# State-space scan and gated feed-forward: where chunks 2 to 5 apply their masked products, and who rearranges C

## The chip, the cores and the metric

The kernel runs on one core of a Trainium2 chip. The metric is the device time of one execution, in microseconds; the time before is the median of three runs. Engines are named as in the profile: PE (TensorE; PEld are its weight loads), DVE (VectorE), ACT (ScalarE), POOL (GpSimd), SP (the engine that issues most DMAs).

## The reference, cut to what matters

Inputs: x (4 batches, 8 heads, 768 positions, 32 wide), a decay a for each batch, head and position, B and C (16 states for each position), and two weight matrices of the feed-forward part (256 x 2048 and 2048 x 256). Everything is float32.

```python
for c in range(nc):                       # chunks along the sequence
    cum = np.cumsum(la, axis=-1)          # la = log(clip(a))
    L = np.exp(cum[:, :, :, None] - cum[:, :, None, :]) * causal
    M = np.einsum('bhin,bhjn->bhij', Cc, Bc) * L
    y_intra = np.einsum('bhij,bhjd->bhid', M, xc)
    y_inter = np.einsum('bhin,bhnd->bhid', Cc, state) * np.exp(cum)[:, :, :, None]
    y[:, :, sl] = y_intra + y_inter
    state = decay_full * state + np.sum(Bx, axis=2)
...
h = x @ w_in          # x: y with its heads side by side, 3072 x 256
g = h * np.cos(h)
out = g @ w_out
```

y of a position is the sum of two parts: what comes from earlier positions of its own chunk, through the causal matrix M, and what comes from the state at the chunk's start.

## The kernel before, in words

**Tiling.** The sequence is cut into six chunks of 128 positions (NC = 6, P = 128), for all four batches at once. Chunks 0 and 1 are done as four units of 64 positions by other functions (`finish0`, `inner`, `weights`); chunks 2 to 5 are done by `turn2`, `intra2`, `masked`, `open2` and `finish2`. The feed-forward part takes each chunk in 16 steps (NF = 16); step n belongs to chunk n // 16.

**A step.** The main loop runs over n. `first(n)` (L725) multiplies 128 features by y into PSUM as hp; `wind` and `gate` (L732, L738, L747) make the cosine on ACT and DVE; `gated` (L752) multiplies it with hp on DVE into gT, and `differ` (L777, L779, L780) forms three differences of gT on POOL. `second(n - 2)`, which is `seven` (L834) from chunk 1 on, multiplies the gT and the differences of two steps before by w_out in seven matmuls. So PE alternates the first of step n with the second of step n - 2. Each engine works through its instructions in the order in which the loop writes them, and semaphores join the engines where a tile is written by one and used by another.

**The scan within the steps.** While the feed-forward part of chunk c - 1 runs, the scan of chunk c is worked in at fixed steps of it (`plan`). Counted from the first step of chunk c - 1: at steps 7 and 11, `turn2` prepares B and C for the two pairs of batches; a step later `intra2` (L621) makes C times B on PE; `masked` (L640) multiplies it on DVE with the decays and writes the masked matrix m, one tile for each batch (`m_at`). m of a batch is 128 rows j (the position that gives) by 8 heads by 128 columns i (the position that receives). The quarter in which j lies in the later half and i in the earlier is never written: it would be zero. The halves of j are laid out so that for the second batch of a pair (s = 1) they change places. The last masked product is written in step 13.

At the end of step 14 `open2` (L651, L659) lays down in the two y tiles the state times C, and in y[0] also the sums from which the next state comes. In step 15, behind the first of that step, `finish2` (L675) adds m times x in two passes: the late columns i over all 128 rows, then the early columns over the 64 rows that count. Then ACT copies y to yT (L682), which the first of step 16 reads, and `carry` (L697 on DVE, L701 on POOL) makes the next state.

**PSUM.** y, g (the result of `intra2`) and a few others share two pairs of banks (tag "scan"). `open2` takes the banks that g held, so it waits for `masked` to have read them.

**Shared tiles.** The tiles `ms` hold other things before chunk 2: parts of them are `lead`, `along1`, `reach1`, `own` and the weights m of the units of chunks 0 and 1.

**The head.** At the start, C of chunk 0 is loaded by four DMAs of the ACT queue as c4. POOL copies it to c0 with its dimensions in another order (L365), PE transposes c0 in four blocks (L417), ACT evicts them (L421) and takes B's transposes behind (L432), and PE makes the first products from them (L478), which DVE multiplies by the decays (L487).

Of the kernel before, what the change touches and what calls it, by code (L numbers as in the profile page):

```python
# [25 lines left out]
def kernel(  # L26
# [13 lines left out]
    V, ACT, G, PE = nc.vector, nc.scalar, nc.gpsimd, nc.tensor  # L40

    NB, H, S, D = x.shape
    N = B.shape[-1]
    P = 128
# [9 lines left out]
    W = P // 2  # L54
# [22 lines left out]
    raw, arow, along, blocks = {}, {}, {}, {}  # L77
# [41 lines left out]
    c4 = both[0][:, 1].rearrange("p (h r) n -> p h r n", h=H)  # L119
# [77 lines left out]
    def load_along(c, seqs=range(NB)):  # L197
# [5 lines left out]
        for b in seqs:  # L203
            for q in range(4 if b % 2 else 1):
# [9 lines left out]
                      in_=a[:, :, 0:P].rearrange("b h (k i) -> (b h) k i", k=2))  # L214
# [85 lines left out]
    for s in range(2):  # L300
# [3 lines left out]
        out=a_in, in_=a.rearrange("(u b) h (c p) -> (b h c) u p", u=NU, p=P))  # L304
# [52 lines left out]
    for p in range(2):  # L357
# [4 lines left out]
                  in_=mine.unsqueeze(2).to_broadcast([P, H, N]))  # L362
    c0 = loads.tile([P, 2, 2, 4, 2, N], FP32, tag="blocks", name="c0").rearrange(
        "p a b c d n -> p (a b c d n)").rearrange("p (r h n) -> p r h n", r=4, h=H)
    G.tensor_copy(out=c0.rearrange("p r h n -> p h r n"), in_=c4)  # L365
    G.memset(lead, 0.0)
    G.memset(lead[:, :, 0:1], 1.0)
    slot = const.tile([P, 2], FP32, name="slot")
# [5 lines left out]
    scaled, lam, reach, state, part, yT = {}, {}, {}, {}, {}, {}  # L374
# [252 lines left out]
    def masked(c, b):  # L627

        u, s = divmod(b, 2)
        g, ms = part[c, u][0:2]  # L630
        l = lam.pop((c, b))
        m = m_at[b]
        first = slice(s * W, s * W + W)
        for q in range(2):
            g_ = g[q][:, ::(-1 if s else 1), s * 2 * P:(s + 1) * 2 * P].rearrange(
                "p k (t i) -> p k t i", t=2)
            m_, l_ = (t[:, q * HH:(q + 1) * HH].rearrange("p (k t) i -> p k t i", k=2)
                      for t in (m, l))
            for js, is_ in ((slice(0, P), slice(W, P)), (first, slice(0, W))):
                V.tensor_tensor(out=m_[js, :, :, is_], in0=g_[js, :, :, is_],  # L640
                                in1=l_[js, :, :, is_], op=ALU.mult)
        ms.append(m)

    def open2(c):

        ys[c] = y = [pair("y") for _ in range(2)]
        for u in range(2):
            for s in range(2):
                for q in range(4):
                    r, p = group(q, s), 64 * (q % 2)  # L650
                    PE.matmul(y[s][p:p + 64, q // 2, u * P:(u + 1) * P],  # L651
                              lhsT=state[c - 1, u][r, s].rearrange("p t d -> p (t d)"),
                              rhs=part[c, u][2][r, s], start=(u == 0), stop=False,
                              tile_position=(r.start, p), skip_group_check=True)
        for b in range(NB if c < NC - 1 else 0):
            x_, sc = raw[c][1], scaled.pop((c, b))
            for q in range(4):
                two_, r = slice(2 * q, 2 * q + 2), group(q, b)
                PE.matmul(y[0][r, 0, (4 + b) * W:(5 + b) * W],  # L659
                          lhsT=sc[:, two_].rearrange("p h n -> p (h n)"),  # L660
                          rhs=x_[:, b, two_].rearrange("p h d -> p (h d)"), start=False, stop=True,
                          tile_position=(0, r.start), skip_group_check=True)

    def finish2(c):

        xr, y = raw[c][1], ys.pop(c)
        for late in (1, 0):
            i = slice(W, P) if late else slice(0, W)
            for u in range(2):
                for t in range(2):  # L670
                    for s in range(2):
                        b, m = 2 * u + s, part[c, u][1][s]
                        js = slice(0, P) if late else slice(s * W, s * W + W)
                        for q in range(4):
                            PE.matmul(y[s][32 * q:32 * q + 32, t, u * P + i.start:u * P + i.stop],  # L675
                                      lhsT=xr[js, b, 4 * t + q], rhs=m[js, 4 * t + q, i],
                                      start=False, stop=True, tile_position=(js.start, 32 * q),
                                      skip_group_check=True)
        yT[c] = two.tile([P, 2, TB], FP32, tag="yT", name="yT")
        to_ = yT[c].rearrange("p t (u s i) -> p t s u i", u=2, s=2)  # L680
        for s in range(2):
            ACT.copy(out=to_[:, :, s],  # L682
                     in_=y[s][:, :, 0:2 * P].rearrange("p t (u i) -> p t u i", u=2))
        for u in range(2):
            del part[c, u]
            if c < NC - 1:
                carry(c, u, y[0][:, 0, 4 * W:].rearrange("p (u s d) -> p u s d", u=2, s=2)[:, u])
# [228 lines left out]
    take_s0, _ = finish0(0)  # L916
# [74 lines left out]
    def pairs(n):  # L991

        return [(c, u) for c, at, _, turn_at, _, _ in plan for u in turn_at
                if at + turn_at[u] == n]
# [9 lines left out]
    def ends(n):  # L1004
        return [(c, us) for c, at, us, _, _, end in plan if at + end == n]
# [61 lines left out]
    for n in range(AHEAD, NC * NF + LAG):  # L1067
        c, f = divmod(n, NF)
        if n < NC * NF:

            if c > 0 and f == (NJ if c == 1 else 0):
                if c == 1:
                    load(2, only=(x,))
                load(c + 2)
            if n in (NF - 4, NF + 1):
                for b in range(2):
                    load_a(2, (2 * (n > NF) + b,))
                    load_along(2, (2 * (n > NF) + b,))
            first(n)
            wind(n)  # L1080
            for at in pairs(n):
                turn2(*at)
            for k in units_at(n, 2):
                turn_unit(k)
            if n + 1 in piece:
                rests_of.append(grade(*piece[n + 1], later=True))
            gate(n)
            while len(rests_of) > (n == AHEAD):
                rest = rests_of.pop(0)
                if rest:  # L1090
                    rest()
            joins = n in piece and piece[n] in held
            if joins:
                join(*piece[n])

            behind = [lambda at=at: halved(*at) for at in halves_at(n)]
            behind += [lambda k=k, p=p: decays0(k, p) for k, at in unit_at.items()
                       for p in range(2) if at[0][p] == n]
            behind = [lambda at=(c, 2 * u + 1): masked(*at) for c, u in pairs(n - 2)] + behind
            behind = [lambda k=k: weights(k, 1) for k in units_at(n - 1, 3)] + behind  # L1100
            if not joins and behind:
                behind.pop(0)()
            gated(n)
            if add_s and (n == NF - 5 or units_at(n - 1, 4)):
                add_s()
                add_s = None
            for do in behind:
                do()
            if f not in (10, 11):
                for do in unsummed:  # L1110
                    do()
                unsummed.clear()
            for k, ((_, last_), *_) in unit_at.items():
                if last_ == n:
                    weigh0(k)
                    if k == 3:
                        units_of_decay()
        for i, js in differ_at.get(n, ()):
            differ_w(i, js)
        for c, _ in ends(n - 1):  # L1120
            finish2(c)
            raw.pop(c)
        if n == AHEAD + 1:
            second(AHEAD - LAG)
        if n >= LAG and n != AHEAD:
            second(n - LAG)
        for c, u in pairs(n - 1):
            intra2(c, u)
            masked(c, 2 * u)
        for k in units_at(n, 3):  # L1130
            for t in range(2):
                inner(k, t)
            weights(k, 0)
        for k in units_at(n, 4):
            take_s, add_s = finish0(k)
            take_s()
        for k in units_at(n, 1):
            reach_unit(k)
        for c, _ in ends(n):
            open2(c)  # L1140
        for c, u in pairs(n + 1):
            for b in (2 * u, 2 * u + 1):
                reaches(c, b)
                load_along(c + 1, (b,))
            turn_blocks(c, u)
        for at, (c, u) in block_loads.items():
            if at == n:
                loading = load_blocks(c, u)
            if at <= n < at + 6:
                next(loading)  # L1150
# [30 lines left out]
```

## Time and profile before

| what | us |
|---|---|
| median of 3 runs (370.49 to 370.82) | 370.5 |
| profiled execution, device time | 371.16 |
| profiled execution, span | 369.4 |
| PE busy | 362.5 |
| DVE busy | 276.9 |
| POOL busy | 213.4 |
| ACT busy | 172.2 |
| L675 PE, four chunks, by the chain | 4 x 1.82 |
| L365 POOL, the copy of C | 0.613 |

The granted clock of PE was 1.0 in the whole profiled execution. Busy times overlap: an engine's busy time says how much it had to do, and only the chain of work that ended last says which of it set the end. Matmul records overlap too, as PE works on several at once, so the time that a group takes is read from the start of its first record to the start of what follows. A float32 matmul leaves two records.

### The profile page before, as it was taken

How to read it: one execution, taken by the hardware profiler on the slowest of the kernel's cores; microseconds unless marked ns; L12 is line 12 of the kernel's file. 1: busy time of each engine (PE TensorE's matmuls, PEld its weight loads, DVE VectorE, ACT ScalarE, POOL GpSimd, SP SyncE). 2: the span in 40 equal slices, each digit the busy share in tenths (PEclk: the TensorE clock that was granted, in tenths of full speed). 3: DMA queues.
4: the chain of work that ended last, by engine and by line, in shares of the span. 5: the costliest groups of instructions: out<-in, count | busy, mean ns of one | idle time of the engine just before them, and what ended most of it. 6: DMA issues, size and time to landing. Idle time of an engine off the chain costs nothing.

```text
span 369.4 us, 9265 instructions
## 1 busy us (share of the span) xinstructions
PE 362.5 (98%) x3646; PEld 325.0 (88%) x3646; DVE 276.9 (75%) x451; ACT 172.2 (47%) x299; POOL 213.4 (58%) x336
## 2 busy tenths in 40 slices
PE   7999999999999999999999999999999999999995
PEld 5688888888999889899989999889999988999995
DVE  7789998578699857978876987776887783543463
ACT  2697766453445244354344344434434534444442
POOL 6567757579784456665446674544675344554451
PEclk9999999999999999999999999999999999999999
DMA  9996957257226736631055341020010010010011
GB/s 135 244 381 134 224 114 100 44 147 185 72 78 90 139 106 91 196 107 34 6 80 113 92 129 44 1 52 5 18 23 0 2 30 2 2 29 2 0 30 30
DMA packets 97708, 30.60 MB, mean 83 GB/s; under 512 B 71456, under 2 KB 93568, under 8 KB 97664
## 3 DMA queue, kind: packets, MB, share of 16 engines
q1 hardware_dynamic: 95376, 29.55, 35.0%
q10 hardware_dynamic: 2288, 0.46, 0.8%
q8 instruction: 29, 0.48, 0.5%
q14 instruction: 15, 0.12, 0.1%
HBM read 26.58 MB, written 3.34 MB: 81 GB/s over the span
## 4 chain that ended last, share of the span: by engine, by line
PE 92%; DVE 3%; ACT 2%; issue 1%; ACTq 0%; DVEq 0%
PE hp L725 43%; PE o L834 34%; PE o L796 6%; PE y L675 2%; PE g L621 2%; DVE mag L279 1%; PE g L478 1%; DVE lam L397 1%; PE warm L84 1%; PE y L651 1%; PE y L520 1%; DVE mag L281 1%; PE y L503 1%; DVE w L738 1%; PE a_ps L386 1%
## 5 line engine op out<-in xcount | busy, mean ns | idle before, releaser
L725 PE MATMUL hp<-yT,w_in 128*128 128x256 f32 x768 | 183.2, 382 | 0.4 <-DVE gT L752 0.3
L725 PEld LDWEIGHTS hp<-yT,w_in 128*128 128x128 f32 x768 | 139.4, 190 | 19.5 <-issue 2.3
L777 POOL TENSOR_TENSOR gd<-gT 128x256 f32<-128x256 f32 x79 | 59.9, 758 | 99.9 <-DVE gT L752 86.8
L747 ACT ACTIVATE w<-w,quarter 128x512 f32<-128x512 f32 x96 | 69.2, 721 | 84.4 <-DVE w L738 84.3
L738 DVE SCALAR_TENSOR_TENSOR w<-hp,k 128x512 f32<-128x512 f32 x96 | 65.8, 685 | 44.3 <-ACT k L732 43.9
L732 ACT ACTIVATE k<-hp 128x512 int32<-128x512 f32 x96 | 57.0, 594 | 83.2 <-PE hp L725 82.9
L752 DVE TENSOR_TENSOR gT<-hp,w 128x512 f32<-128x512 f32 x96 | 65.3, 680 | 33.2 <-ACT w L747 21.7
L834 PE MATMUL o<-words,gd 128*128 128x128 f32 x474 | 66.0, 275 | 0.0
L834 PEld LDWEIGHTS o<-words,gd 128*128 128x128 f32 x474 | 59.3, 192 | 0.3 <-POOL gd L779 0.2
L834 PEld LDWEIGHTS o<-w_out,gT 128*128 128x128 f32 x316 | 47.2, 191 | 4.2
L834 PE MATMUL o<-w_out,gT 128*128 128x128 f32 x316 | 48.4, 276 | 0.0
L779 POOL TENSOR_TENSOR gd<-gT,gd 128x128 f32<-128x128 f32 x79 | 44.0, 556 | 6.2
L780 POOL TENSOR_TENSOR gd<-gT,gd 128x128 f32<-128x128 f32 x79 | 43.3, 548 | 6.2
L580 DVE TENSOR_TENSOR_SCAN lam<-arow,unit 128x512 f32<-128x512 f32 x32 | 42.7, 1333 | 0.0
L834 PE MATMUL o<-words,gT 128*128 128x128 f32 x158 | 30.6, 275 | 0.0
L834 PE MATMUL o<-w_out,gd 128*128 128x128 f32 x158 | 30.5, 275 | 0.0
L796 PE MATMUL o<-w_out,gT 128*128 128x256 f32 x128 | 29.9, 379 | 0.0
L796 PEld LDWEIGHTS o<-w_out,gT 128*128 128x128 f32 x128 | 24.2, 190 | 3.3
L640 DVE TENSOR_TENSOR m<-g,lam 128x256 f32<-128x256 f32 x64 | 24.7, 414 | 0.4
L834 PEld LDWEIGHTS o<-words,gT 128*128 128x128 f32 x158 | 24.0, 192 | 0.0
L834 PEld LDWEIGHTS o<-w_out,gd 128*128 128x128 f32 x158 | 24.0, 192 | 0.0
L851 DVE TENSOR_TENSOR sum<-ps,sum 128x256 f32<-128x256 f32 (+1 forms) x27 | 16.7, 645 | 0.6
(111 smaller groups left out, 279.2 us busy)
## 6 DMA issues: line engine op xcount, KB each, us to landing
arow<-a_cut SPq DMA_DIRECT2D x16, 512.0 KB
words<-in_moe_w_in_dram SPq DMA_DIRECT2D x8, 512.0 KB
words<-in_moe_w_out_dram SPq DMA_DIRECT2D x8, 512.0 KB
out_dram<-sum SPq DMA_DIRECT2D x18, 128.0 KB
xr<-in_x_dram SPq DMA_DIRECT2D x16, 128.0 KB
xr<-in_x_dram SPq DMA_DIRECT2D x16, 64.0 KB
bc<-in_B_dram SPq DMA_DIRECT2D x15, 64.0 KB
arow<-a_cut SPq DMA_DIRECT2D x2, 256.0 KB
```

Of the source, the lines that this page charges most:

```text
L580: V.tensor_tensor_scan(out=lam[c, b][:, hs].rearrange("p h i -> p (h i)"), data0=rows_.rearrange("p h i -> p (h i)"), data1=unit[:, b % 2 ...
L640: V.tensor_tensor(out=m_[js, :, :, is_], in0=g_[js, :, :, is_], in1=l_[js, :, :, is_], op=ALU.mult)
L725: PE.matmul(to_[:, e], lhsT=w_in[:, k, fs], rhs=y[:, k], start=(k == 0), stop=(k == KT - 1), skip_group_check=True)
L732: ACT.activation(k, hp[n], AF.Copy, bias=0.25, scale=INV_2PI)
L738: V.scalar_tensor_tensor(out=w, in0=hp[n], scalar=INV_2PI, in1=k, op0=ALU.mult, op1=ALU.subtract)
L747: ACT.activation(cos, cos, AF.Sin, bias=quarter, scale=TWO_PI)
L752: V.tensor_tensor(out=gT[n], in0=hp.pop(n), in1=cos, op=ALU.mult)
L777: G.tensor_tensor(out=d[:, 0:2], in0=g[:, 1:2].to_broadcast([P, 2, P]), in1=g[:, 3::-3], op=ALU.subtract)
L779: G.tensor_tensor(out=d[:, 2], in0=g[:, 0], in1=d[:, 0], op=ALU.subtract)
L780: G.tensor_tensor(out=d[:, 3], in0=g[:, 2], in1=d[:, 2], op=ALU.subtract)
L796: PE.matmul(o[c, u][:, t], lhsT=g[:, 2 * e + t], rhs=w_out[:, 2 * j + e], start=(j == e == t == 0), stop=(j == NJ - 1 and e == 1), skip_gr ...
L834: PE.matmul(at[q], lhsT=a_[q], rhs=w[q], start=(j == 0 and q in starts), stop=(j == NJ - 1), skip_group_check=True)
```

## The change

The scan and the head are edited. In `finish2` the two passes of 64 matmuls of 64 columns become one pass of 32 matmuls of 128 columns over all 128 rows, zeros included; so that the unwritten quarter of m holds zeros, `masked` sets it to zero once, in chunk 2, by a POOL memset for each batch (the quarter is not written again by any later chunk). And `finish2` is called directly behind `open2`, at the end of step 14, in place of step 15. In the head, the copy from c4 to c0 is cut in two: POOL copies the first two of four blocks, ACT the other two.

```diff
-    G.tensor_copy(out=c0.rearrange("p r h n -> p h r n"), in_=c4)
+    G.tensor_copy(out=c0[:, 0:2].rearrange("p r h n -> p h r n"), in_=c4[:, :, 0:2])
+    ACT.copy(out=c0[:, 2:4].rearrange("p r h n -> p h r n"), in_=c4[:, :, 2:4])
...
         m = m_at[b]
+        if c == 2:
+            G.memset(m[W - s * W:P - s * W, :, 0:W], 0.0)
...
-        for late in (1, 0):
-            i = slice(W, P) if late else slice(0, W)
-            for u in range(2):
-                for t in range(2):
-                    for s in range(2):
-                        b, m = 2 * u + s, part[c, u][1][s]
-                        js = slice(0, P) if late else slice(s * W, s * W + W)
-                        for q in range(4):
-                            PE.matmul(y[s][32 * q:32 * q + 32, t, u * P + i.start:u * P + i.stop],
-                                      lhsT=xr[js, b, 4 * t + q], rhs=m[js, 4 * t + q, i],
-                                      start=False, stop=True, tile_position=(js.start, 32 * q),
-                                      skip_group_check=True)
+        for u in range(2):
+            for s in range(2):
+                for h in range(H):
+                    q, t = h % 4, h // 4
+                    PE.matmul(y[s][32 * q:32 * q + 32, t, u * P:(u + 1) * P],
+                              lhsT=xr[:, 2 * u + s, h], rhs=part[c, u][1][s][:, h],
+                              start=False, stop=True, tile_position=(0, 32 * q),
+                              skip_group_check=True)
...
-        for c, _ in ends(n - 1):
-            finish2(c)
-            raw.pop(c)
         if n == AHEAD + 1:
...
         for c, _ in ends(n):
             open2(c)
+            finish2(c)
+            raw.pop(c)
```

## The prediction

> **What bounds the kernel now.** I read the engines' rows of the page first, then the chain of work that ended last, then the timeline at one of the four places that are edited, then the head of the kernel.
>
> ```profile
> PE 362.5 (98%) x3646; PEld 325.0 (88%) x3646; DVE 276.9 (75%) x451; ACT 172.2 (47%) x299; POOL 213.4 (58%) x336
> PE 92%; DVE 3%; ACT 2%; issue 1%; ACTq 0%; DVEq 0%
> L675 PE MATMUL y<-m,xr x512: 212/219/243, 131.5 to 307.5; 128*32 128x64 f32 x86, 64*32 64x64 f32 x85
> ```
>
> TensorE is busy for 98% of the span and is 92% of the chain, so a change counts by what it does to the order and the seams of TensorE's work; other engines count only if TensorE comes to wait for them. The third line is the edited code: 512 records, 128 in each of chunks 2 to 5 (a float32 matmul leaves two records). The next lines are the passage of chunk 3, from the timeline (start, duration, engine, line, records; durations overlap, so I subtract starts).
>
> ```profile
> 186.99 0.69 PE L651 MATMUL y<-rT,state 32*64 32x128 f32 x32
> 187.61 0.65 PE L659 MATMUL y<-xr,sc 128*32 128x64 f32 x32
> 188.19 1.99 PE L725 MATMUL hp<-yT,w_in 128*128 128x256 f32 x8
> 190.12 1.89 PE L675 MATMUL y<-m,xr 128*32 128x64 f32 x128
> 191.94 0.71 PE L834 MATMUL o<-w_out,gT 128*128 128x128 f32 x4
> 193.60 1.89 PE L725 MATMUL hp<-yT,w_in 128*128 128x256 f32 x8
> ```
>
> By starts: L651 0.62, L659 0.58, the first of step 15 1.93, L675 1.82, the second behind it 1.66, with no stall. Elsewhere the chain gives a first 1.73 (eight records of 216 ns) and a second 1.56 (fourteen of 111 ns), so leaving the small tiles costs the next large group 0.20 and 0.10. Inside L675, counting records begun by a given time (PE busy and count are the fields behind the comma):
>
> ```profile
> 189.10:190.20 1.10, 0.08 (x5) 1.00 0.66 65
> 189.10:191.00 1.90, 0.88 (x63) 1.00 0.78 75
> 189.10:191.10 2.00, 0.98 (x64) 1.00 0.75 73
> 189.10:191.80 2.70, 1.68 (x128) 1.00 0.71 72
> ```
>
> The first 64 records (late columns, 128 rows) start 14 ns apart; then about 0.12 us passes with one new start; the last 64 (early columns, 64-row tiles) take about 0.68, 10.6 ns each; then 0.17 until L834 starts.
>
> **The change: finish2's matmuls.** 64 matmuls of 64 columns become 32 of 128 columns over 128 rows, 64 records a chunk. Four column groups work side by side: the late half shows that, since 14 ns times four is the 56 ns of one 64-column record. Price of a new record: 111 ns (L834, same columns) over four, 27.8 ns; the bounds are 27.0 (half of L725's 216 ns for 256 columns, over four) and 28.2 (twice the late record). From first to last start 63 x 27.8 = 1.75 us. So nothing is won in streaming: the early half did 64 rows in tiles of their own and now streams the zero rows too.
>
> A rule speaks against this edit: the Trainium skill, "TensorEngine Tiling (Array Packing)", Tiling Modes, lists eight independent tiles of 64x32 and four of 128x32. By it the early half would run at 7 ns a record, 0.45 us, and giving it up would cost 0.23 a chunk, 0.9 in all, more than my sum. The row says 10.6 ns, 0.68 us; I use the row. The same section says that a change of tiling mode drains TensorE. Here it bears on the sum: the row shows 0.12 inside L675 and 0.16 to 0.19 from the last start of a small group to the next group. Six changes of mode a chunk become three (large, 32x64, 128x32, large), and L659 joins L675 without one. By count alone, three times 0.12 to 0.19 would be 0.36 to 0.57 a chunk; the sum by starts gives less, because part of it pays for the longer stream (1.75 against 0.90 and 0.68) and the exit behind 128 columns is longer (0.21: L651's 0.19 and a little):
>
> L659's last start 188.03; L675's first 188.08 (0.05 for a semaphore, the 51 ns that the row of L675 shows for its own); last 189.83; first of step 15 at 190.04; second at 191.97; next first 193.53. Before it was 193.60: **0.07 saved**, 0.21 with chunks 2 and 4. Chunk 5 has no L659: 303.23 + 0.43 + 0.19 + 1.75 + 0.21 + 1.90 + 1.56 = 309.27, the start that it has now: **0**. If the seam is free and a record takes 27.0 ns, a chunk saves 0.17; if a record takes 28.2 and the seam is a drain of 0.19, it loses 0.1. Four chunks: -0.21, bounds -0.6 and +0.4.
>
> **The move.** finish2 goes from behind the first of step 15 to behind open2. It needs the masked products of step 13; open2 already waits for those, since its y takes the banks that they free: their last DVE instruction (L640) ends at 186.78, 0.2 before L651. So no new wait there. In chunk 2 it ends at 128.28 and L651, begun at 127.83, halts about half a microsecond; that remains.
> The first of step 15 now starts 1.85 later. Behind it: k at 192.1, w at 192.7, a scan, then gT about 195.3 and differences on GpSimd until 197.2; second of step 15 needs them at 198.5, so 1.3 us of cover. On ScalarE the two copies to yT (L682, 0.53 each by starts) come ahead of k(15), in the time when there is no hp: hidden, and the first of step 16, which now finds them done at 193.32 and starts at 193.60, gets 2 us more. On VectorE carry (L697) comes ahead of w(15); its second pair waits for GpSimd's L701, which stands behind the differences of step 14 (begun at 189.79, 1.8 us), so until about 192.1, and w(15) queues behind. It is ready only at 192.7: hidden, with 0.2 left; beyond that the 1.3 above. open2 and finish2 issue no DMA; SP isn't passed by anything that waits, as the loads into the freed x buffer come a chunk later.
>
> **The zeros.** Chunk 2 adds four GpSimd memsets of 64 x 512. The nearest row:
>
> ```profile
> L366 POOL MEMSET m<- 128x260 f32 x1 | 0.3, 319 | 0.0
> masks.py:197 POOL MEMSET ident<- 128x128 f32 x1 | 0.2, 205 | 0.3 <-POOLq L1165 0.3
> 108.54 1.39 DVE L640 TENSOR_TENSOR m<-g,lam 128x256 f32<-128x256 f32 x4
> 113.05 0.73 POOL L777 TENSOR_TENSOR gd<-gT 128x256 f32<-128x256 f32 x1 [2.10 <-DVE gT L752]
> 129.15 0.73 POOL L777 TENSOR_TENSOR gd<-gT 128x256 f32<-128x256 f32 x1 [4.60 <-DVE gT L752]
> ```
>
> About 0.86 ns an element, so 0.54 each; up to 1.3, as L779 goes from 0.46 to 1.25 beside a VectorE scan. Two fall in the idle 2.10 us before 113.05, two in the 4.60 before 129.15: **0**, if only finish2 waits for them.
>
> **The copy of C.** GpSimd's one copy (0.61) becomes halves on two engines.
>
> ```profile
> 6.62 0.61 POOL L365 COPY c<-bc 128x512 f32<-128x512 f32 x1 [0.84 <-DMA bc<-in_C_dram]
> 7.29 0.66 PE L417 MATMUL tp<-ident,c 128*128 128x128 f32 x4 [0.50 <-POOL c L365]
> 7.98 0.84 ACT L421 ACTIVATE cT<-tp,slot 128x256 f32<-128x256 f32 x2 [3.33 <-DVE lam L397]
> 9.14 0.73 PE L478 MATMUL g<-cT,turned 32*64 32x128 f32 x32 [0.54 <-ACT turned L432]
> 9.87 1.29 DVE L487 TENSOR_TENSOR m<-g,lam 128x512 f32<-128x512 f32 x2 [0.54 <-PE g L478]
> ```
>
> C lands at about 6.6. A half costs GpSimd 0.40 (between 0.29 for 128 elements and 0.61 for 512), ScalarE 0.38 to 0.45 (its copies of 128x256 take 0.375 out of PSUM). ScalarE has nothing else: behind the copy stand only the evictions of the same transposes. So L417 starts about 0.2 earlier, and L421, L478 and L487 with it; L421's named releaser (a scan ending at 7.98) is no operand of it, its transposes end at 7.95. L487 can gain up to its 0.54. Until the steady stage at 35 us the chain is engine behind engine. **-0.20**; bounds 0 (the scan does release L421, or a later arrival absorbs it) and -0.3.
>
> **Sum** against the profiled execution: span 369.4 - 0.21 - 0.20 = 368.99; what lies around the span (1.76 to its 371.16) is untouched. The same 0.41 off the median of 370.5 is 370.09: **370.1 us**, a ratio of 0.9989.
>
> **Rivals.**
> *More is gained*, 369.6: free seams (0.6) and a head of 0.3. For it: the drains are seen; against: the longer exit. Chance 0.22.
> *The copy brings nothing*, 370.3 to 370.5: L421 is named as waiting for the scan. Against: no operand. Chance 0.13.
> *The zeros hold VectorE back*, slower: if the masked products of chunk 2 must wait for the memset of their tile, because the two patterns interleave, they wait at 108.54 for GpSimd, whose memset stands behind differences that end at 110.95, until 111.5: 2.96 us. gT(25) moves from 112.9 to 115.9 and its differences with it, while the second that uses them stands at 115.27; its third product has 0.6 of cover. It decides from there: 2.3 lost, another 0.54 where open2 of chunk 2 already halts, less 0.41: 372.9. Against it, weights were loaded from w_in while GpSimd wrote an interleaved slice of it:
>
> ```profile
> 51.27 1.28 POOL L289 TENSOR_TENSOR w_in<-mag,last 128x512 uint32<-128x512 uint32 x1 [0.63 <-DVE mag L281]
> 50.90:52.35 1.45, 0.38 (x3) 1.00 0.53 123
> ```
>
> The third weight load begins by 52.35, before the write ends at 52.55, and its columns lie between the two runs being written. Chance 0.13.
> *The forecast*, 369.7 to 370.5: 0.52.
>
> **Range and chances.** 0.2% is 0.74 us, about what a measurement of this kernel can tell from no change. Faster takes the first rival and 0.06 of the forecast: 0.28. Slower takes the zeros and 0.04 for a stall I don't see: 0.17. The rest, 0.55, is the same. The range 369.3 to 371.3 leaves out the zeros and the ends.
>
> **What would show it.** Right: L675 with 64 records a chunk, about 1.75 from first to last start, directly behind L659 within 0.06; first of step 15 near 2.0 after L675's start; L417 near 7.1; memsets near 0.54 in GpSimd's idle time. Wrong: L640 of chunk 2 idle behind a memset; records over 28.2 ns, so the tiles don't overlap at 128 columns; TensorE idle before a second of step 14 or 15; L478 still at 9.14.

## The result and the profile after

| what | before | after |
|---|---|---|
| median, side by side (11 runs each), us | 370.81 (370.43 to 371.8) | 369.59 (369.14 to 370.17) |
| ratio | | 0.9968 (95%: 0.9959 to 0.9977) |
| span of the profiled execution, us | 369.4 | 368.0 |
| PE records | 3646 | 3390 |

The changed kernel is 1.2 us faster, 0.3%. The forecast was 0.41 us. The range holds the result, but the likeliest case was a third of what came, and the time is that of the first rival, "more is gained" (chance 0.22). By the prediction's own line of 0.2% the result is not "the same" but faster, to which it gave 0.28.

The page of the changed kernel: the engines' busy time and instructions, the chain that ended last by engine, and the queue that brings instructions.

```profile
PE 361.3 (98%) x3390; PEld 325.4 (88%) x3390; DVE 276.2 (75%) x451; ACT 173.0 (47%) x300; POOL 217.6 (59%) x340
PE 91%; DVE 3%; DMA 2%; ACT 2%; issue 1%; SPq 1%; ACTq 0%
q8 instruction: 27, 0.44, 0.5%
```

TensorE is still the bound, with 256 records fewer: 64 instead of 128 in each of four chunks. POOL has four instructions more (the zeros) and ACT one (its half of the copy). The last line plays a part below: instructions come in packets, 27 here and 29 before.

The passage of chunk 3, from the timelines (start, duration, engine, line, records): of the kernel before, the first of step 14, whose start the prediction does not show, and then of the changed kernel, from the first of step 14 to that of step 16:

```profile
183.60 1.89 PE L725 MATMUL hp<-yT,w_in 128*128 128x256 f32 x8
```

```profile
182.91 1.89 PE L724 MATMUL hp<-yT,w_in 128*128 128x256 f32 x8
...
186.29 0.69 PE L654 MATMUL y<-rT,state 32*64 32x128 f32 x32
186.92 0.65 PE L662 MATMUL y<-xr,sc 128*32 128x64 f32 x32
187.39 1.93 PE L674 MATMUL y<-m,xr 128*32 128x128 f32 x64
189.25 1.99 PE L724 MATMUL hp<-yT,w_in 128*128 128x256 f32 x8
191.08 0.61 PE L833 MATMUL o<-w_out,gT 128*128 128x128 f32 x4
...
192.64 1.89 PE L724 MATMUL hp<-yT,w_in 128*128 128x256 f32 x8
```

Six line numbers have moved: open2 is L654 and L662, finish2 L674, the first L724, the second L833. The new order is there: finish2 stands directly behind open2. Subtracting starts as the prediction did: L654 0.63, from L662 to L674 0.47, L674 1.86, the first of step 15 1.83, the second 1.56. From the first of step 14 to that of step 16 it is 6.34 + 3.39 = 9.73; before, the same two starts lay 193.60 - 183.60 = 10.00 apart.

Inside L674, the stretches that count records begun by a given time (the field in brackets; PE's busy time ahead of it):

```profile
186.40:187.45 1.05, 0.06 (x4) 1.00 0.18 41
186.40:188.40 2.00, 1.01 (x40) 1.00 0.54 75
186.40:189.10 2.70, 1.71 (x64) 1.00 0.52 67
```

Thirty-six records in 0.95 us are 26.4 ns each. Four column groups do overlap at 128 columns, a little better than the lower bound that I gave (27.0).

**Where the 1.4 us of the spans went.** I took the distance from the first of a chunk's step 14 to that of its step 16 in both traces, and the two steps 36 and 37 of the loop (3.29 each where nothing disturbs them; the expectation of `e5_same` below counts differently and calls them 35 and 36):

| stretch | before | after | difference |
|---|---|---|---|
| chunk 2 | 5.12 + 5.41 | 6.92 + 3.39 | -0.22 |
| chunk 3 | 4.59 + 5.41 | 6.34 + 3.39 | -0.27 |
| chunk 4 | 4.59 + 5.41 | 6.34 + 3.39 | -0.27 |
| chunk 5 | 4.05 + 5.38 | 5.89 + 3.39 | -0.15 |
| steps 36 and 37 | 3.47 + 3.62 | 3.29 + 3.29 | -0.51 |

That is -0.91 for the four passages and -0.51 in two steps that lie between the first passage and the second. The head gives nothing in this pair of executions: open2 of chunk 2 begins at 127.83 before and at 127.86 after.

**The head.** From the timeline of the changed kernel:

```profile
6.47 0.41 ACT L366 COPY c<-bc 128x256 f32<-128x256 f32 x1 [1.69 <-DMA bc<-in_C_dram]
6.50 0.40 POOL L365 COPY c<-bc 128x256 f32<-128x256 f32 x1 [0.71 <-DMA bc<-in_C_dram]
6.96 0.66 PE L418 MATMUL tp<-ident,c 128*128 128x128 f32 x4
7.65 0.84 ACT L422 ACTIVATE cT<-tp,slot 128x256 f32<-128x256 f32 x2 [0.77 <-PE tp L418]
8.80 0.73 PE L479 MATMUL g<-cT,turned 32*64 32x128 f32 x32 [0.54 <-ACT turned L433]
11.44 0.37 PE L513 MATMUL y<-xr,sc 64*32 64x64 f32 x20 [0.60 <-DMA xr<-in_x_dram]
```

The two halves run side by side in 0.40 us in place of 0.61, the transposes begin 0.33 earlier (C also landed a little earlier) and the products L479 0.34 earlier. Then TensorE waits 0.60 for x, whose load was late in this execution, and the lead is gone.

**Zeros, VectorE and carry.** From the timelines of POOL and DVE in chunk 2, and of DVE behind the first of step 15 in chunk 3:

```profile
111.03 1.09 POOL L635 MEMSET m<- 64x512 f32 x2
124.69 1.09 POOL L635 MEMSET m<- 64x512 f32 x2
```

```profile
108.57 1.40 DVE L643 TENSOR_TENSOR m<-g,lam 128x256 f32<-128x256 f32 x4
124.70 1.40 DVE L643 TENSOR_TENSOR m<-g,lam 128x256 f32<-128x256 f32 x4
191.31 0.47 DVE L696 SCALAR_TENSOR_TENSOR whole<-state,reach,y 128x64 f32<-128x64 f32 x2 [1.27 <-POOL state L700]
191.97 0.69 DVE L737 SCALAR_TENSOR_TENSOR w<-hp,k 128x512 f32<-128x512 f32 x1 [0.18 <-ACT k L731]
```

The memsets take 518 ns each in time in which POOL was idle. The first masked products of chunk 2 have no wait in brackets: at 108.57 they begin although the memset of their tile begins only at 111.03. Carry waits 1.27 for POOL, as foreseen, and ends early enough: w of step 15 waits 0.18 for ACT's k, not for carry.

### The profile page after: what moved, and what is told of

The parts are those of the page before. It is cut to its first block, busy times and chain, and to the rows that moved or that the text cites. A ratio compares the mean times of both kernels' runs of the same rounds, so it can differ in the third digit from the quotient of the medians.

```text
span 368.0 us, 8760 instructions
## 1 busy us (share of the span) xinstructions
PE 361.3 (98%) x3390; PEld 325.4 (88%) x3390; DVE 276.2 (75%) x451; ACT 173.0 (47%) x300; POOL 217.6 (59%) x340
## 3 DMA queue, kind: packets, MB, share of 16 engines
HBM read 26.58 MB, written 3.34 MB: 81 GB/s over the span
## 4 chain that ended last, share of the span: by engine, by line
PE 91%; DVE 3%; DMA 2%; ACT 2%; issue 1%; SPq 1%; ACTq 0%
PE hp L724 44%; PE o L833 34%; PE o L795 6%; DMA xr<-in_x_dram 2%; PE y L674 2%; PE g L622 2%; DVE mag L279 1%; PE y L654 1%; PE y L521 1%; DVE mag L281 1%; PE g L479 1%; PE y L504 1%; DVE w L737 1%; PE o L878 1%; ACT mag L266 0%
## 5 line engine op out<-in xcount | busy, mean ns | idle before, releaser
L724 PE MATMUL hp<-yT,w_in 128*128 128x256 f32 x768 | 183.2, 382 | 0.3 <-DVE gT L751 0.3
L724 PEld LDWEIGHTS hp<-yT,w_in 128*128 128x128 f32 x768 | 139.3, 190 | 19.9 <-issue 3.2
L833 PE MATMUL o<-words,gd 128*128 128x128 f32 x474 | 65.9, 275 | 0.0
L833 PEld LDWEIGHTS o<-words,gd 128*128 128x128 f32 x474 | 59.3, 192 | 0.0
L833 PEld LDWEIGHTS o<-w_out,gT 128*128 128x128 f32 x316 | 47.5, 191 | 4.0
L779 POOL TENSOR_TENSOR gd<-gT,gd 128x128 f32<-128x128 f32 x79 | 46.0, 582 | 6.2
L833 PE MATMUL o<-w_out,gT 128*128 128x128 f32 x316 | 48.0, 274 | 0.0
L778 POOL TENSOR_TENSOR gd<-gT,gd 128x128 f32<-128x128 f32 x79 | 44.0, 556 | 6.2
L833 PE MATMUL o<-words,gT 128*128 128x128 f32 x158 | 30.6, 275 | 0.0
L833 PE MATMUL o<-w_out,gd 128*128 128x128 f32 x158 | 30.5, 275 | 0.0
L643 DVE TENSOR_TENSOR m<-g,lam 128x256 f32<-128x256 f32 x64 | 24.7, 414 | 0.4
L833 PEld LDWEIGHTS o<-w_out,gd 128*128 128x128 f32 x158 | 24.0, 192 | 0.0
L833 PEld LDWEIGHTS o<-words,gT 128*128 128x128 f32 x158 | 24.0, 192 | 0.0
L850 DVE TENSOR_TENSOR sum<-ps,sum 128x256 f32<-128x256 f32 (+1 forms) x27 | 16.6, 640 | 0.6
```

The lines of the kernel that those rows point to most:

```text
L724: PE.matmul(to_[:, e], lhsT=w_in[:, k, fs], rhs=y[:, k], start=(k == 0), stop=(k == KT - 1), skip_group_check=True)
L778: G.tensor_tensor(out=d[:, 2], in0=g[:, 0], in1=d[:, 0], op=ALU.subtract)
L779: G.tensor_tensor(out=d[:, 3], in0=g[:, 2], in1=d[:, 2], op=ALU.subtract)
L833: PE.matmul(at[q], lhsT=a_[q], rhs=w[q], start=(j == 0 and q in starts), stop=(j == NJ - 1), skip_group_check=True)
```

## The experiments

Two theories stood at the start: that of the forecast (a small gain in the passages and a part from the head, as in the sum by starts), and that the seams count for more than the sum gave them, so that the scan's edits explain nearly all. The twelve runs tell apart the copy, the move, the merged pass and the zeros, and then what the move alone brought to light.

**The copy alone** (`e1_head`).

```diff
-    G.tensor_copy(out=c0.rearrange("p r h n -> p h r n"), in_=c4)
+    G.tensor_copy(out=c0[:, 0:2].rearrange("p r h n -> p h r n"), in_=c4[:, :, 0:2])
+    ACT.copy(out=c0[:, 2:4].rearrange("p r h n -> p h r n"), in_=c4[:, :, 2:4])
```

> Only the copy of C is shared by GpSimd and ScalarE; the scan is as before. Theory A (the prediction's step): 0.20 us faster, ratio 0.9995, with the first products of the scan (L478 of before) some 0.2 earlier and first(0) with them. Theory B (from the trace of after): the products start 0.3 earlier, but the next matmuls wait for the load of x, so first(0) isn't earlier and nothing is gained: ratio 1.000 within 0.0005.

Measured: 370.92 (11 runs) against 371.27 (26 runs); ratio 0.9992 (0.9984 to 1.0001). In us that is -0.3, between -0.6 and 0: the forecast's 0.20 fits, and so does nothing. In its trace C landed at 5.96, before TensorE was free for the transposes (6.87), so the copy was not what they waited for. Where C lands late, as above, the copy's 0.2 is real but can be taken back by x. The start of the copy, which waits for C to land, moves by 0.9 us between executions (5.77 to 6.66 in the traces here), more than what the copy is worth. Away from the head this trace differs from that of before in two places: steps 36 and 37 take 3.29 + 3.49, 0.31 less, and the passage of chunk 5 takes 0.20 more.

**The scan's edits alone** (`e2_scan`): the changed kernel with the copy of C as it was.

```diff
-    G.tensor_copy(out=c0[:, 0:2].rearrange("p r h n -> p h r n"), in_=c4[:, :, 0:2])
-    ACT.copy(out=c0[:, 2:4].rearrange("p r h n -> p h r n"), in_=c4[:, :, 2:4])
+    G.tensor_copy(out=c0.rearrange("p r h n -> p h r n"), in_=c4)
```

> The whole edit of the scan (one pass of finish2, its place behind open2, the zeros), with the copy of C on GpSimd alone as before. Theory A: 0.21 us faster, ratio 0.9994. Theory B (starts in the trace of after): 0.26 a chunk in chunks 2 to 4 and 0.14 in chunk 5 are saved between the state times C and the first of step 16, 0.87 in all, ratio 0.9977, and all of what the change gained but 0.3 at most.

Measured: 370.10 (8 runs), ratio 0.9969 (0.9959 to 0.9980), where the whole change gives 0.9968. So the gain is the scan's, as far as medians with 0.4 us of uncertainty can say. Its trace has the same four passages as the changed kernel, and 3.34 + 3.36 in steps 36 and 37 (0.12 over the undisturbed 6.58, against 0.51 before).

**The move alone** (`e3_move`): finish2 with its two passes, directly behind open2; no zeros.

```diff
-        for c, _ in ends(n - 1):
-            finish2(c)
-            raw.pop(c)
...
             open2(c)
+            finish2(c)
+            raw.pop(c)
```

> finish2 stands behind open2, but keeps its two passes (64 matmuls of 64 columns, late columns over 128 rows, early ones over 64); no zeros are written, and the copy of C is on GpSimd alone. If what pays is the number of changes of tiling and of visits (theory B): nearly all of the gain, 0.87 us, ratio 0.9977; a chunk takes 6.35 to 6.4 from the start of the state times C to the first of step 16, as in after. If fewer and longer matmuls are what pays (theory C): at most a third of it, 0.3, ratio 0.9992.

Measured: 374.28 (6 runs, 372.88 to 376.06), ratio 1.0083 (1.0058 to 1.0108): **slower**. Its timeline, chunk 3 and then the places in chunks 4 and 5 where finish2 is interrupted:

```profile
187.27 0.69 PE L651 MATMUL y<-rT,state 32*64 32x128 f32 x32
188.37 1.86 PE L675 MATMUL y<-m,xr 128*32 128x64 f32 x128
190.16 1.99 PE L725 MATMUL hp<-yT,w_in 128*128 128x256 f32 x8
...
246.15 1.31 PE L675 MATMUL y<-m,xr 128*32 128x64 f32 x68
247.81 0.81 PE L675 MATMUL y<-m,xr 64*32 64x64 f32 x60 [0.35 <-issue]
...
304.07 1.84 PE L675 MATMUL y<-m,xr 128*32 128x64 f32 x122
307.34 0.31 PE L675 MATMUL y<-m,xr 64*32 64x64 f32 x6 [1.43 <-issue]
```

Where nothing disturbs it, in chunk 3, the move saves more than the whole change: the two steps take 9.66 there, against 10.00 before and 9.73 after. L675 itself takes 1.79 (188.37 to 190.16), 0.03 less than in its old place. But in chunk 4 TensorE halts after 68 of the 128 records, and in chunk 5 after 122, with "issue" in the brackets: it waits for nothing that the profile shows. The profiled execution, the fastest of the six, adds up: its span of 371.1 is 1.7 over that of before. Its open2 of chunk 2 begins 0.59 later (128.42), behind a wait of 0.85 for VectorE at 56.5 that the second trace of this kernel does not show, and its passages of chunks 2 to 5 change by -0.32, -0.34, +0.27 and +1.48: 1.68 together. (The brackets count only from the end of the last record, which overlaps others; the passages are longer by 0.61 and 1.70 than without the halts.) Both theories failed on this run: neither had halts.

**The merged pass alone** (`e4_merge`): one pass of 128 columns with the zeros, finish2 in its old place behind the first of step 15.

```diff
+        if c == 2:
+            G.memset(m[W - s * W:P - s * W, :, 0:W], 0.0)
...
-        for late in (1, 0):
-            i = slice(W, P) if late else slice(0, W)
...
+        for u in range(2):
+            for s in range(2):
+                for h in range(H):
+                    q, t = h % 4, h // 4
+                    PE.matmul(y[s][32 * q:32 * q + 32, t, u * P:(u + 1) * P],
+                              lhsT=xr[:, 2 * u + s, h], rhs=part[c, u][1][s][:, h],
...
```

> finish2 in one pass of 32 matmuls of 128 columns with zeros, but in its old place in step 15, behind the first; the copy of C is on GpSimd alone. Theory B: nothing gained, since the stream gets 0.15 longer and one drain of 0.12 falls away: ratio 1.000 within 0.0007. Theory C: most of the gain, 0.6 or more, ratio 0.9984 or below.

Measured: 370.81 (11 runs), ratio 0.9992 (0.9984 to 1.0001). Its timeline in chunk 3:

```profile
188.70 1.99 PE L723 MATMUL hp<-yT,w_in 128*128 128x256 f32 x8
190.63 1.96 PE L673 MATMUL y<-m,xr 128*32 128x128 f32 x64
192.51 0.71 PE L832 MATMUL o<-w_out,gT 128*128 128x128 f32 x4
```

The pass takes 1.88 in place of 1.82. The passages cost 0.06 more in chunks 3 to 5 and 0.11 in chunk 2; steps 36 and 37 take 3.34 + 3.36, so 0.39 comes back there. The two runs add up in the passages: in chunk 3 the move is worth -0.34 and the merged pass +0.06, together -0.28, and the whole change shows -0.27. So in the passages **the whole gain is the move's**, and the merged pass costs a little. What it does for the move is the next question.

**The kernel before against itself** (`e5_same`), no edit.

> The kernel before, unchanged, against itself: ratio 1.000 within 0.0005. In its trace the two steps of chunks 2 to 5 around the first of step 15 take 10.53, 10.00, 10.00 and 9.43 us again, to 0.05. Open: whether the 0.5 us by which steps 35 and 36 (counted by groups of first) took longer in the trace of before come again. If they belong to the order of the instructions they do, to 0.1; if they are scatter of that execution they differ by more.

Measured: 370.69 (11 runs) against 370.96 (21 runs), ratio 0.9998 (0.9989 to 1.0007). The profiled span was 368.7, where the other execution of the same kernel had 369.4: single spans differ by 0.7 us by what happens in the head. The passages, and the 3.47 + 3.62 of steps 36 and 37, are the same in both, so these differences belong to the kernel and not to an execution.

**The zeros made to hold VectorE** (`e6_held`): one column more is set to zero, which the first masked product then writes, so that VectorE must wait for POOL.

```diff
-            G.memset(m[W - s * W:P - s * W, :, 0:W], 0.0)
+            G.memset(m[W - s * W:P - s * W, :, 0:W + 1], 0.0)
```

> The changed kernel, with each memset one column wider, so that it overlaps what the masked product writes next (which overwrites that column) and VectorE waits for GpSimd in chunk 2. This is the third rival of the prediction made true. By its working: VectorE is held 3.0 us ahead of the first masked product and 0.54 ahead of the third, TensorE loses 2.3 in a second of step 9 and 0.54 at open2 of chunk 2, so 2.8 us over the changed kernel: 372.5 to 373, ratio to before 1.005. If VectorE makes up for the delay before TensorE asks: under 1 us over the changed kernel, ratio below 0.9995.

Measured: 373.54 (5 runs) against 370.96, ratio 1.0071 (1.0058 to 1.0085); the span is 371.7, 3.7 over the changed kernel's. From its timeline:

```profile
110.94 1.12 POOL L635 MEMSET m<- 64x520 f32 x2
111.51 1.41 DVE L643 TENSOR_TENSOR m<-g,lam 128x256 f32<-128x256 f32 x4 [2.95 <-POOL m L635]
114.69 0.71 PE L833 MATMUL o<-w_out,gT 128*128 128x128 f32 x4 [2.59 <-ACT ps L842]
```

The rival's mechanism exists and the wait has its size: VectorE is held 2.95 us for the memset (2.96 in the prediction). What follows took another way. The second that halts is the one at 112.10, not the one at 115.27, and what it waits for is a PSUM bank: ACT's copies of the last o stand behind a cosine that VectorE now gives it late. That costs 2.86 in step 26, and 0.71 in the passage of chunk 2: 3.6, where the prediction had 2.3 + 0.54. In the changed kernel no such wait appears, so this rival is out because it did not happen, not because it is cheap.

**The zeros in every chunk** (`e8_each`): sixteen memsets in place of four.

```diff
-        if c == 2:
+        if c >= 2:
```

> The changed kernel, with the four memsets in each of chunks 2 to 5 in place of chunk 2 alone: twelve more of 0.54 on GpSimd. By the prediction's step they are hidden in GpSimd's idle time and only finish2 waits for them, with microseconds to spare: the same as the changed kernel, ratio to before 0.997. If GpSimd's time is on the path anywhere near: up to 1.6 us over it, ratio 1.001.

Measured: 369.41 (4 runs), ratio 0.9960 (0.9946 to 0.9973), against 0.9966 for the changed kernel in `e7_after`, on another chip. Twelve memsets more cost nothing that can be measured: they are hidden.

**The changed kernel again** (`e7_after`), no edit against it, and **the move alone again** (`e9_again`), no edit against `e3_move`, to see whether the halts stay in place.

> The changed kernel once more, on the same chip as the run with the sums moved: ratio to before 0.997, its two steps around open2 10.31, 9.73, 9.73 and 9.28 in chunks 2 to 5, and no halt inside finish2.

> The same kernel as in the run with finish2 behind open2 in two passes, once more. If the halts inside finish2 come from where the blocks of TensorE's instructions end, they come again in chunks 4 and 5 and not in chunks 2 and 3, with lengths that may differ. If they are scatter, they come in other chunks.

Measured: the changed kernel 369.48 (5 runs), ratio 0.9966 (0.9953 to 0.9978), passages of 10.31, 9.73, 9.73 and 9.28 and no halt in any. The move alone: 372.33 (5 runs), ratio 1.0040 (1.0022 to 1.0058), and in its timeline

```profile
245.46 1.31 PE L675 MATMUL y<-m,xr 128*32 128x64 f32 x68
247.86 0.81 PE L675 MATMUL y<-m,xr 64*32 64x64 f32 x60 [1.09 <-issue]
...
306.83 0.31 PE L675 MATMUL y<-m,xr 64*32 64x64 f32 x6 [0.87 <-issue]
```

The halts come after the same records (68 and 122) and have other lengths (1.09 and 0.87, where they were 0.35 and 1.43). A place that is fixed in the instruction stream, and a length that varies, speak for the supply of instructions: a block that comes by DMA and is late. (Here the two halts lengthen their passages by 1.35 and 1.13.)

**The stream shifted by half a block** (`e10_shift`): the move alone, with 32 one-column matmuls (64 records, each with its weight load) among the warm-up matmuls at the start. The trace has the packets of the instruction queue at 16,384 bytes. TensorE's entries in it (two for a record, its weight load and its multiply, and one for a semaphore wait) are 7415 for 29 packets before and 6903 for 27 after, so one packet is 256 of them by estimate, and 64 records with their weight loads are half of it.

```diff
-    fill(bank([P, 2, P], "warm", "o"), 1)
+    shift = bank([P, 2, P], "warm", "o")
+    fill(shift, 1)
+    for _ in range(32):
+        PE.matmul(shift[:, 0, 0:1], lhsT=ones, rhs=ones[:, 0:1], start=True, stop=True,
+                  skip_group_check=True)
```

> The same, with 32 matmuls of one column (64 records, 128 instructions of TensorE, half a block of 16 KB) added in the warm-up at the start, where they cost under 1 us. If the halts inside finish2 come from the supply of instructions, the passages of chunks 2 to 5 now lie half a block further on, and the halts leave chunk 5 or change place within it, and others may appear in chunks 2 or 3. If the halts come from anything in the order of the work itself (a bank, a wait for VectorE), they stay where they were, in chunks 4 and 5 behind the same records.

Measured: 389.53 (2 runs), since the added records take 13.5 us at the head (3.77 to 17.28), far more than expected of them; only the places of the halts are read. From its timeline, chunks 2, 3 and 4:

```profile
144.63 1.43 PE L675 MATMUL y<-m,xr 128*32 128x64 f32 x88
147.18 0.65 PE L675 MATMUL y<-m,xr 64*32 64x64 f32 x40 [1.11 <-issue]
...
204.26 1.72 PE L675 MATMUL y<-m,xr 128*32 128x64 f32 x110
207.32 0.38 PE L675 MATMUL y<-m,xr 64*32 64x64 f32 x18 [1.35 <-issue]
...
265.42 1.13 PE L725 MATMUL hp<-yT,w_in 128*128 128x256 f32 x4
267.51 1.13 PE L725 MATMUL hp<-yT,w_in 128*128 128x256 f32 x4 [0.96 <-issue]
```

In chunk 4 the halt moves from 68 records behind the start of finish2 to 132 (its 128, and four of the first): exactly 64, half a block, so that the direction makes no difference. Chunk 5 has none now, and chunks 2 and 3, which had none, halt after 88 and 110 records. Nothing in the work of the passages changed; its place in the stream did. I also numbered TensorE's entries from the start of each trace. The first entry that comes late is 5313 and 6593 in the move alone, both times, and 3009, 4289 and 5569 in the shifted kernel: each is 193 past a multiple of 256. **The halts come where one block of instructions ends and the next is not there yet.** In the three traces the stream goes on 2.2 to 2.8 us after the start of the instruction packet that precedes it (packet at 245.6, stream at 247.81 in the first).

A block of 128 records at 14 ns is 1.8 us of work. In the move alone, 160 to 192 small records stand in a row; TensorE halts where a block ends behind 132 or more of them (the block held 1.8 to 2.3 us of work), and not where it ends behind 111 or fewer, as in chunks 2 and 3. The merged pass has half the records, at 26.4 ns: open2 and finish2 together are 128 records, and from the first start to the last 2.76 us pass (186.29 to about 189.05). In neither trace of the changed kernel (`after`, `e7_after`) is there a halt of this kind. In the kernel before, the eight large records of the first (1.93 us) stand between open2 and finish2. Even so, the trace of the copy alone, which has this order, has a gap of 0.19 in finish2 of chunk 5, at entry 6593 again: that is its 0.20.

How much of this the merged pass owes to the place of its blocks is not shown. In the changed kernel the only block end close behind all 128 records of a passage falls in the first behind chunk 4, 3.7 us after the block end before it. It is free there in the changed kernel, but in `e6_held`, whose TensorE stream is the same, that first is held 0.18 (2.01 in place of 1.83), at entry 5057, again 193 past a multiple of 256. A block made of a passage alone would be about 2.8 us of work, and no shifted version of the changed kernel was run.

The Trainium skill, "Runtime: NRT & Kernel Launch", Instruction fetch mechanics, says the same of the block (16 KiB, 256 instructions, fetched by the engine's own DMA queue while the one before runs), and that the fetch is mostly hidden, because instructions are issued more slowly than they come. Here it is not hidden: by the rule the move alone should have kept its gain in every chunk; by the rows TensorE stood idle for 0.35 to 1.43 us at a halt.

**The sums of VectorE moved out of chunk 2's way** (`e11_sums`, `e12_sums1`). In the changed kernel chunk 2 is the passage with a halt left (10.31 in place of 9.73): open2 waits for masked products that VectorE finishes late, behind the sums of step 12. In `e11_sums` the four sums that VectorE does in step 12 of every chunk move to step 15; in `e12_sums1` only those of chunk 1's feed-forward part, in which this happens.

```diff
-            if f not in (10, 11):
+            if f not in (10, 11, 12, 13, 14):
```

```diff
-            if f not in (10, 11):
+            if f not in (10, 11) and not (c == 1 and f in (12, 13, 14)):
```

> The changed kernel, with the four sums of the feed-forward part that VectorE does in step 12 (2.3 us, ahead of the masked products of the second pair) moved to step 15. In chunk 2 TensorE halts about half a microsecond inside the state times C because these products are late. If that is their only cause: 0.5 us faster than the changed kernel, ratio to before 0.9955; open2 to first of step 16 of chunk 2 then as in chunk 3. If the sums are late for something in step 15 or the first of the next chunk: no gain or a loss, with a halt of TensorE in steps 15 to 18 of each chunk.

> The changed kernel, with the four sums of step 12 moved to step 15 in chunk 1's steps alone (the passage of chunk 2), where moving them took away TensorE's halt, and left in step 12 in the later chunks; the last of these had lost 1.7 us at the end. Expected: 0.58 us faster than the changed kernel, the two steps around open2 of chunk 2 taking 9.73 in place of 10.31 and the last stretch 10.8, ratio to before 0.995. If the gain is made up elsewhere: as the changed kernel, 0.997.

Measured: `e11_sums` 370.79 (11 runs), ratio 0.9995 (0.9986 to 1.0004): chunk 2 gains 0.58, but the kernel's last stretch takes 12.49 in place of 10.78, with the last chunk's sums (L850, begun at 361.37) now close ahead of the last additions (L867, at 363.17).

`e12_sums1`: 368.87 (5 runs, 368.77 to 369.37), ratio 0.9954 (0.9941 to 0.9968), 0.61 below the changed kernel on the same chip (369.48). Its chunk 2, from the timeline:

```profile
127.37 0.69 PE L654 MATMUL y<-rT,state 32*64 32x128 f32 x32
128.00 0.65 PE L662 MATMUL y<-xr,sc 128*32 128x64 f32 x32
```

L654 is one piece of 32 records, 0.63 to the next; the passage is 6.34 + 3.39 like that of chunk 3. This version beats both kernels.

## Why the prediction was right in direction and short in size

**finish2's matmuls, the seam: right in each term but two.** The entry from open2 to finish2 took the forecast 0.47, the exit 0.20 (0.21), the second 1.56. Two terms were mis-sized. The step that failed first is "first of step 15 at 190.04; second at 191.97": it kept the 1.93 that this first took before. The prediction read the 0.20 by which it exceeds 1.73 as the price of leaving small tiles alone. Half of it was for going back into them behind, a change of tiling that the move takes away: the trace has 1.83, and where small tiles still follow, in `e4_merge`, the same first takes 1.93 (188.70 to 190.63). The other is the price of a record, 27.8 ns: it is 26.4, below the bounds, so the pass from first start to first of step 15 is 1.86 and not 1.96. Together 0.20 a chunk: the forecast of 0.07 becomes the measured 0.27. In chunk 5 the same two terms make 0.15 out of 0. I had also worked out the seams by count (0.36 to 0.57 for three) and set it aside for the sum by starts. The move alone takes away two changes of tiling where no halt disturbs it and saves 0.34, 0.17 each; in chunk 5, which has no L659, it takes away one and saves 0.22 (`e10_shift`, 5.82 + 3.39 against 4.05 + 5.38). So the count was the better guide, and the sum had kept a seam that was gone.

**The rule on tiles: the row was rightly preferred.** With the move alone the two passes take 1.79, and one pass 1.86 behind it. Giving up the eight small tiles costs 0.06 to 0.07 a chunk net of the seam inside L675 that goes with them, and the early records start 10.6 ns apart, not the 7 that the rule would have made.

**What the merged pass is for: missed.** The prediction weighed it by the streaming time alone and found nothing won. That is right for the stream, and `e4_merge` shows it. But without it the move loses to halts more than it wins, and with it, in the stream as it lies, there are none. The trace before shows no halt of this kind, so the prediction could not have had its size; the number of records in a row was in it.

**Steps 36 and 37: not foreseen, 0.5 of the gain.** From the chain of waits before, and then after:

```profile
151.60 1.97 PE hp L725 x8
153.57 1.82 PE o L834 x14
```

```profile
151.40 1.73 PE hp L724 x8
153.13 1.56 PE o L833 x14
```

These two groups need 1.73 and 1.56, and took 1.97 and 1.82. They wait for the bank of hp and for the differences, because VectorE's adds (L851) and gT lie late. Part of it begins with ACT's k of step 34, from the timelines of ACT before, after, and in the copy alone:

```profile
143.81 0.60 ACT L732 ACTIVATE k<-hp 128x512 int32<-128x512 f32 x1 [0.64 <-PE hp L725]
```

```profile
143.36 0.60 ACT L731 ACTIVATE k<-hp 128x512 int32<-128x512 f32 x1 [0.36 <-PE hp L724]
143.41 0.60 ACT L733 ACTIVATE k<-hp 128x512 int32<-128x512 f32 x1 [0.36 <-PE hp L726]
```

That k starts 2.27 behind the start of its first in the kernel before, and 1.99 in the changed kernel, while ACT is idle. The wait for hp isn't the cause: it is over 0.32 before k starts in the kernel before, and 0.04 in the changed one. The lateness goes with the edit of the head: all seven traces in which POOL copies the whole of C have it, none of the seven in which ACT copies half. The copy itself is long over by then (6.9), but it and its wait put two entries more ahead of this k in ACT's stream. Counted like TensorE's, ACT's entries 191 and 319 start 0.32 late in all of the seven, 128 apart, and 191 is this k.

The differences on POOL tell the same of the zeros. POOL's entry 196, the first difference of a step, starts 0.38 behind the end of its wait for gT, in place of the usual 0.09 to 0.11, in twelve of the fourteen traces (in `e11_sums` and `e12_sums1` POOL is busy up to then). Without the four memsets ahead this entry belongs to step 35, and TensorE waits 0.18 for that step's differences in step 37 (at 154.00 in the kernel before). With them it belongs to step 34, and TensorE does not wait.

| steps 36 and 37, over the undisturbed 6.58 | without zeros, finish2 in two passes | with zeros, one merged pass |
|---|---|---|
| POOL copies all of C | 0.51 (before, also with the move alone) | 0.12 (`e4_merge`, `e2_scan`) |
| ACT copies half | 0.20 (`e1_head`) | 0 (after) |

So each of the two edits takes something away, and the move nothing. What the late entries have in common is their place in an engine's stream, as with TensorE's halts. That they too wait for a block of instructions fits, but no run moved these places alone. The 0.51 is more than the whole forecast, and no term of the prediction had it.

**The copy of C: right in mechanism, not measurable in time.** The halves took 0.41 and 0.40 (0.38 to 0.45 and 0.40 were forecast), the releaser of L422 is now TensorE, so the scan named before was no operand, and the products came 0.34 earlier. The step that didn't hold is that this reaches the end: in the profiled execution x took it back, and the copy alone measures -0.3 with 0 inside the interval. What its trace does show, 0.31 less in steps 36 and 37, comes by a way that the prediction did not have.

**The move's neighbours and the zeros: right.** Copies to yT and carry hid where they were said to; w waited 0.18 for k; the memsets took 518 ns (0.54) in POOL's idle time; L643 had no wait. The rival of the zeros was right in kind and dearer than said, by a bank and not by the differences.

**By the numbers:** of -1.4 between the spans, 0.21 was forecast for the passages and is 0.91; 0.20 for the head and is about 0; nothing for steps 36 and 37 and is 0.51. The median says -1.2. So the rival "more is gained" had the time, its free seams (0.6) for the most part, and not its head of 0.3; that its 0.9 came so close was luck, since 0.5 came from steps that it does not name, by the place of instructions in their streams. The range held for its width, not because the sum behind its middle was right.

## What to carry to other kernels

When a group of small-tile matmuls is moved, count every change of tiling that goes away on both sides, in the large group's own time too: here each was worth about 0.2 us, and part of it was hidden in the duration of the large group between the small ones. Then count the records that stand in a row without a large matmul between them: with 160 to 192 of them TensorE was halted wherever a block of 256 instructions ended behind 132 or more, and that cost more than the seams gave. A merged pass that wins nothing in streaming may be what makes the move possible. And compare two traces away from the edit too: an instruction more in an engine's stream can shift something far behind it.

## What the runs showed of the hardware that I had not expected

- TensorE can halt for want of instructions in straight code: 0.35 to 1.43 us at a time, after the same record in repeated executions of one kernel, and always 193 entries past a multiple of 256 in its stream, also when 64 records are put in front.
- Records of 128 columns over four column groups start 26.4 ns apart, where the same columns over the whole array take 111 ns (27.8 for a quarter).
- One-column float32 matmuls over the whole array are not cheap in a row: 64 records more in the warm-up took 13.5 us, 0.21 us each, at a granted clock of 1.00.
- Two executions of the same kernel differ by 0.7 us in their profiled span, and by as much in when C lands in the head (6.62 and 5.92), which is more than an edit of the head was worth.
- One instruction more on ACT, at 6.5 us, goes with a k that starts 0.28 earlier behind its first, some 137 us later: it splits all fourteen traces, seven and seven. The late entries of ACT are 191 and 319 of its stream.
